# Two layers of experts behind an attention: weights of the first layer moved behind the slots' transposes, zero rows written one at a time, attention's tail a turn further ahead

## Chip, core and metric

The kernel runs on one core of a Trainium2 chip. The metric is the device time of one execution in microseconds; the kernel before takes 1737.48 us, the median of three runs (1734.93 to 1743.86). The engines are TensorE (PE; its weight loads are PEld), VectorE (DVE), ScalarE (ACT), GpSimd (POOL) and SyncE (SP). Each runs its own instructions in order; SP issues nearly all DMAs here, POOL the indirect ones.

## The reference

Three stages of 24576 tokens with 128 features each: an attention against 768 pooled keys, and two mixtures of eight experts that pick one expert per token.

```python
# attention, q (2, 12288, 128), kv (2, 384, 32, 128)
kv_pool = kv.reshape(B, H // 4, 4, W // 4, 4, C).mean(axis=(2, 4))
k = v = kv_pool.reshape(B, -1, C) @ w_sr            # 768 keys of each batch
s = (q @ k.transpose(0, 2, 1)) / sqrt(C)
a = exp(s - max(s)); a /= a.sum(-1) + 1e-9
x = (a @ v).reshape(B * S, D)
# layer 1
logits = x @ w_gate
e = argmax(logits); gate = softmax(logits)[e]
x = gate * (relu(x @ w1[e]) @ w2[e])                # F = 1024
# layer 2: the same, with logits = cosine(x, expert_emb) / tau and its own w1, w2
```

## The kernel before

**Attention** runs over 48 groups of 512 tokens. Its work is written as a list `plan` of entries `operation:lag`; in turn n an entry does its operation for group n - lag. The letters that matter here are `K` (scores, line 531), `N` (row maximum), `E` (exponential), `S` and `Z` (high and low half of the probabilities in fp16), `t` (DMA transpose on SP, line 568), `A` (product with v, lines 575 to 577), `R` (product with `iwg`: output and logits, line 603), `p` (one small step of the routing, whose last four steps are scatters of rows by POOL, line 491) and `ul`, `ua`, `ug`, `uw`, which prepare layer 1's expert weights. The largest lag is 6, so the last group is done in turn 53.

**Routing.** Each token's row (its value as two fp16 halves, its gate and its number) is scattered into an HBM table `xs` at a row that belongs to its expert. For each layer two tables of slots are made on the chip (`table`, kinds "a" and "b"); kind "b" also writes 512 zero rows behind the last row of each expert (`zrows`, line 799), eight writes of 260 KB. A table is a generator that takes one step at each `.` of the plans (eight in a slot's turn), or all at once when a slot needs it.

**Slots.** A slot is 512 (a few times 256) rows of one expert, 50 in layer 1 and 51 in layer 2, numbered from 1 in the instructions' names (x0_9 is the ninth, of layer 0 in the program's counting). A slot's work is in three lists, `both`, `plan_1` and `plan_2`, each cut into eight parts by "/"; entries are merged by their position in a turn. `X` loads a slot's rows by a DMA transpose (`x`, line 930), `W0` and `W1` load its weights (line 868; skipped at run time where the buffer holds the expert already), `H` and `h`, `g` are relu(x w1) for one of eight blocks of 128 hidden features (TensorE lines 955 to 957, ScalarE 960, VectorE 965), `Y` the second product (974 to 976), `p` the steps after it. In layer 1 these begin with the two halves of the result and two DMA transposes of them (`rowss`, line 1000); `n` are the norms: POOL adds the transposed halves (line 1012), ScalarE squares them (line 1017).

**Weights.** Expert weights are prepared in five phases: load the raw fp32 weights into `wraw` (`pw_load`, two DMAs of 512 KB, lines 340 and 341), square both halves (ScalarE, line 350), take a power of two from the sums, split each half into fp16 high and low parts in `whl` (ScalarE line 358, VectorE line 374), store them (`pw_store`, lines 383 and 385, 1 MB). `wraw` and `whl` have one buffer each. Layer 1's experts 0 to 4 are done during attention, 5 to 7 during the slots, by the entries `vl`, `va`, `vg`, `vs` of `plan_1`, and layer 2's eight after them; for layer 2 only the scales are stored, and the slots split the weights themselves.

**The seam.** Attention's last turns run among the first slots: after each entry of the slots' lists the program emits attention's entries up to position `n0 + i + m / len(plan_l) + DN` (in turns, n0 = 48, `DN` = 0). Four rules force attention further where a PSUM bank is shared: slot 0's `H0` waits for the last `E`, `Y0` and `p` of the first slots for the last `x`, `l` and `w`; `upto` then emits all entries up to that one at once. The order in which the program emits instructions is the order in which each engine runs them.

Of the kernel before, what the change touches and what calls it, by code (L numbers as in the profile page):

```python
# [66 lines left out]
def moe_kernel(tc, q, kv, w_sr, w_gate, w1a, w2a, emb, tau, w1b, w2b, out):  # L67
    with ExitStack() as ctx:
        _body(ctx, tc, q, kv, w_sr, w_gate, w1a, w2a, emb, tau, w1b, w2b, out)


def _body(ctx, tc, q, kv, w_sr, w_gate, w1a, w2a, emb, tau, w1b, w2b, out):
# [272 lines left out]
    def pw_square(i, k):  # L345
        raw = pw[i][0]
        if k == 0:
            pw[i][1] = sm.tile([P, 2], F32, tag="wss", name=f"wss{i}", bufs=2)
            pw[i][3] = p1.tile([P, WC], F16, tag="whl", name=f"whl{i}")
        A.activation(pw[i][3].bitcast(BF16)[:, 0:F], raw[:, k, :], AF.Square, accum_out=pw[i][1][:, k:k + 1])  # L350

    def pw_act(i, ph):
        raw, ss, sc, hl = pw[i]
        if ph == 1:
            pw_square(i, 1)
        elif ph in (3, 4) and i < E:
            k = ph - 3
            A.activation(hl[:, 2 * F * k:2 * F * k + F], raw[:, k, :], AF.Copy, scale=sc[:, k:k + 1])
# [18 lines left out]
    def pw_store(i, ph):  # L377
        if ph == 0:
            pw_square(i, 0)
        if ph == NPH - 1:  # L380
            l, e = divmod(i, E)
            _, _, sc, hl = pw.pop(i)
            ins = [SP.dma_start(WS[l][e * P:(e + 1) * P, :], sc).ins]
            if l == 0:
                ins.append(SP.dma_start(WT[e * P:(e + 1) * P, :], hl).ins)
                if e >= EA:
                    for w in ins:
                        for r in w_reads:
                            tc.declare_no_dep(w, r, reason="weights of other experts")
                    w_late.extend(ins)  # L390
# [248 lines left out]
    def at_u(g, fn):  # L639

        i, ph = divmod(g - U0, UP)
        if 0 <= i < EA and ph % UW == 0 and ph // UW < NPH:
            fn(i, ph // UW)


    def table(info, l, kind, ns, nh=0, prev=None, left=None):
# [24 lines left out]
        def slots_of(lim):  # L671

            cmp = tt([P, E, NG], "cmp")
            n = tt([P, E], f"n{lim}")
            V.scalar_tensor_tensor(cmp, todo.unsqueeze(2).to_broadcast([P, E, NG]), float(-lim),
                                   kidx.unsqueeze(1).to_broadcast([P, E, NG]), op0=ALU.add, op1=ALU.is_gt)
            yield
            V.tensor_reduce(n, cmp, axis=AX.X, op=ALU.add)
            yield
            return n  # L680
# [63 lines left out]
        n = yield from slots_of({"a": TG - 0.5, "b": TG // 2, "c": 0}[kind])  # L744
# [51 lines left out]
        if kind != "a":  # L796
            for e in range(E):
                r = sp_val(bi[0:1, e:e + 1], NROW - TG)
                ins = SP.dma_start(XS[l].rows[bass.ds(r, TG), :].rearrange("(p r) c -> p r c", r=4), zrows)
                XS[l].wrote(ins.ins)  # L800
                if e % 2:
                    yield
            info["upto"] = XS[l].mark()
        if kind == "b":
            lf = tt([P, E], "lf")
# [17 lines left out]
    def sp_val(ap, hi):  # L823
        return nc.values_load(ap, engines=[mybir.EngineType.SP], min_val=0, max_val=hi,
                              skip_runtime_bounds_check_because=SKIP)
# [312 lines left out]
    for n, ((i, w0, m), t) in enumerate(zip(parts, tl)):  # L1138
# [13 lines left out]
        if n == 6:  # L1152
# [7 lines left out]
    steps = {"q": at_q, "Q": at_Q, "qH": at_qH, "qL": at_qL, "K": at_K, "N": at_N, "E": at_E, "S": at_S, "D": at_D,  # L1160
             "Z": at_Z, "t": at_t, "A": at_A, "x": at_x, "r": at_r, "R": at_R, "w": at_w, "l": at_l, "o": at_o, "p": at_p,
             "ul": lambda g: at_u(g, pw_load), "ua": lambda g: at_u(g, pw_act),
             "ug": lambda g: at_u(g, pw_dve), "uw": lambda g: at_u(g, pw_store)}
    plan = """
        q:0 K3:3 ul:0 S1:3 p:6 Z3:4 E2:3 p:6 p:6 A5:5 qL:2 p:6 . ua:0 N3:3 t2:4 p:6 ug:0 w1:6 x:5 o0:6 Q:1 p:6 K0:2
        p:6 o1:6 Z1:3 R0:5 N0:2 t0:3 E3:3 R1:5 p:6 p:6 S2:3 t3:4 E0:2 S0:2 kd:1 kg:0 . l0:5 l1:5 K1:2 r0:3 Z2:3 p:5
# [15 lines left out]
    def at_turn(n):  # L1182

        for m, x in enumerate(plan):
# [24 lines left out]
            if 0 <= g < NG and not (g == 0 and o in ("Q", "qH", "qL")) and not (o == "q" and g < 3):  # L1209
                steps[o](g) if k is None else steps[o](g, k)  # L1210
                done.add((g, o, k))
                if o == "p" and g == G_A - 1 and NA1 and st[g]["post"].gi_frame is None and "l" not in taba:
                    taba["l"] = 0
                    side.append(table(taba, 0, "a", NA1))
                    tick()
                yield m

    def pw_all(steps_):
        for i in steps_:
            for fn in (pw_load, pw_act, pw_dve, pw_store):  # L1220
                fn(*divmod(i, NPH))

    def turns(slots, hooks, after, first_part=None):
# [46 lines left out]
    def run(*a):  # L1270
        for _ in turns(*a):
# [2 lines left out]

    lsteps = {"X": slot_load, "f": slot_mark, "W": slot_w, "H": slot_h, "h": slot_hH,
              "g": slot_hL, "Y": slot_y, "B": slot_raw, "C": slot_hi, "D": slot_lo}
    wsteps = {"vl": pw_load, "va": pw_act, "vg": pw_dve, "vs": pw_store}

    both = """
        Y3:3 h6:3 H7:3 g6:3 . / Y4:3 h7:3 H0:2 g7:3 . / Y5:3 h0:2 H1:2 g0:2 . / Y6:3 h1:2 H2:2 g1:2 . /  # L1280
        Y7:3 h2:2 H3:2 g2:2 f:2 . / Y0:2 h3:2 H4:2 g3:2 . / Y1:2 h4:2 H5:2 g4:2 . / Y2:2 h5:2 H6:2 g5:2 ."""
    plan_1 = """
        - - p:5 p:4 n:5 - p:4 p:4 / W0:1 n:4 p:5 p:4 n:5 - p:5 p:4 p:5 p:4 / X:1 vl:0 p:5 n:5 - p:5 n:4 vg:1 n:4 p:4 /
        - n:4 p:5 n:4 - p:4 p:4 p:4 / - n:4 p:5 - p:4 - vs:1 / p:3 W1:1 n:4 p:5 - - n:4 /
        - p:3 p:3 n:4 p:3 - n:4 va:0 n:4 / - n:4 p:3 - n:4 p:4 - n:4"""
    plan_2 = """
        - - p:4 - D3:2 / - - - - / - - p:4 - X:1 / - - - - C0:1 p:4 / - - - - D0:1 C1:1 / p:3 - - p:3 - - D1:1 /
        - - B0:0 - C2:1 - D2:1 / - - B1:0 - C3:1 -"""
# [11 lines left out]
    def first(info, l, n):  # L1300
        return lambda: side.append(table(info, l, "a", n))

    def rest(info, l, n_a, prev=None, left=None):
        side.append(table(info, l, "b", NG - n_a, NH[l], prev.get("rows") if prev else None,
                          left["left"] if left else None))
# [8 lines left out]
            before[e] = ins  # L1314

    last_a = NG + max(lags)
    DN = 0

    along = NA1 and NA2

    def late():
        if not NA1:
            pw_all(range(min(NPH * E, max(0, NG - U0)), NPH * E))
        if not along:
            pw_all(range(NPH * E, 2 * NPH * E))
# [22 lines left out]
    if NA1:  # L1348
# [8 lines left out]
        def upto(what):  # L1357
            nonlocal pos
            while what not in done:
                pos = next(rest_)  # L1360

        for i, m, j, o in turns(slots, hooks, after, NPH * E if along else None):
# [7 lines left out]
            if j == 0 and o == "p":  # L1370
                upto((NG - 1, "l", 1))
                upto((NG - 1, "w", 1))
            while pos < (n0 + i + m / len(plan_l) + DN) * len(plan):
                pos = next(rest_, 1 << 30)
# [5 lines left out]
    n = nc.values_load(tab2b["count"][0:1, 0:1], min_val=0, max_val=2 * NT, skip_runtime_bounds_check_because=SKIP)  # L1380
# [31 lines left out]
```

## Time and profile before

| what | value |
|---|---|
| median of three runs | 1737.48 us |
| profiled execution, its own time | 1748.93 us |
| its span, first to last instruction | 1747.2 us |
| busy: PE, DVE, ACT, POOL | 1594.9, 1441.0, 1328.0, 982.0 us |
| mean granted TensorE clock | 0.975 |
| DMA | 240.61 MB, mean 138 GB/s |

The profile is one execution; the span is 1.7 us shorter than the execution's time. A busy share is a mean over stages, so the rows below go by stretches of the span, in us from its start: attention until about 600, its tail among the first slots until about 690, layer 1's slots until about 1230, layer 2's slots to the end. A matmul's duration in the trace includes its pipeline, so a slot's time is better taken from the distance of slot starts than from the sum of its matmuls. A wait is put down to the last of the things waited for.

### The profile page before, as it was taken

The page shows a single profiled execution, that of the slowest core. Times are in us where ns is not written, and L with a number is a line of the kernel's source. Part 1 is how long each engine was busy: PE and PEld are TensorE (multiplying, and loading weights), DVE is VectorE, ACT ScalarE, POOL GpSimd, SP SyncE. Part 2 cuts the span into 40 slices and gives each one's busy share as a digit, 9 for nine tenths or more (in the row PEclk, how much of TensorE's full clock was granted, in tenths as well). Part 3 has the DMA queues.
Part 4 walks back from the last instruction along what each step waited for, and adds up shares of the span by engine and source line. Part 5 has one row for each costly group of instructions (what it writes and reads, how often), then busy time and mean ns, then how long its engine had stood idle before and what let it go on. Part 6 is the DMA issues. An engine that isn't in the chain of part 4 may idle for free.

```text
span 1747.2 us, 31671 instructions
## 1 busy us (share of the span) xinstructions
PE 1594.9 (91%) x8713; PEld 890.4 (51%) x8713; DVE 1441.0 (82%) x3887; ACT 1328.0 (76%) x2731; POOL 982.0 (56%) x1298
## 2 busy tenths in 40 slices
PE   6888988989888789899999999998999999999996
PEld 6666656656666534444444444444444444444443
DVE  5898989989899757787788787787998888888875
ACT  3777778878777746776777877776888888888885
POOL 1386665665565646565666666665544444444453
PEclk9899999999999999999999999999999999999998
DMA  7999998999999953444665455445337335343353
GB/s 247 218 236 201 173 225 174 207 209 179 218 181 190 189 108 78 110 109 113 145 160 123 98 112 106 74 95 128 76 77 175 78 76 127 75 83 74 77 121 63
DMA packets 631019, 240.61 MB, mean 138 GB/s; under 512 B 578464, under 2 KB 604202, under 8 KB 629168
## 3 DMA queue, kind: packets, MB, share of 16 engines
q1 hardware_dynamic: 611776, 200.31, 57.5%
q0 software_dynamic: 18752, 38.18, 8.2%
q8 instruction: 70, 1.15, 0.3%
q14 instruction: 117, 0.96, 0.2%
q10 hardware_dynamic: 304, 0.01, 0.0%
HBM read 148.53 MB, written 52.02 MB: 115 GB/s over the span
## 4 chain that ended last, share of the span: by engine, by line
PE 57%; DVE 18%; issue 8%; DMA 7%; ACT 6%; POOL 3%; SPq 0%; POOLq 0%; ACTq 0%; DVEq 0%
PE ps L957 7%; PE ps L955 7%; PE ps L974 7%; PE ps L956 7%; PE ps L976 7%; PE ps L975 7%; PE ps L531 5%; DVE hL L965 4%; DMA aT<-ab 3%; DVE ab L561 3%; DMA rowss<-yHLs 2%; DVE nm L538 2%; PE ps L575 2%; ACT ab L552 2%; PE ps L577 2%
## 5 line engine op out<-in xcount | busy, mean ns | idle before, releaser
L965 DVE SCALAR_TENSOR_TENSOR hL<-ps,hH 128x512 f16<-128x512 f32 (+1 forms) x808 | 540.0, 672 | 168.6 <-ACT hH L960 114.6
L960 ACT ACTIVATE hH<-ps 128x512 f16<-128x512 f32 (+1 forms) x808 | 466.7, 584 | 174.4 <-PE ps L957 144.2
L1075 POOL DMA_INDIRECT out_dram<-rowss,idxs x198 | 211.4, 1068 | 258.9 <-DVE idxs L1072 157.7
L974 PE MATMUL ps<-hH,wbuf 128*128 128x512 f16 (+1 forms) x808 | 304.1, 376 | 7.3 <-ACT hH L960 7.1
L491 POOL DMA_INDIRECT xs<-rowsa,idxa x192 | 202.6, 1055 | 189.5 <-DVE sca L431 143.1
L976 PE MATMUL ps<-hL,wbuf 128*128 128x512 f16 (+1 forms) x808 | 303.9, 376 | 1.3
L975 PE MATMUL ps<-hH,wbuf 128*128 128x512 f16 (+1 forms) x808 | 304.0, 376 | 0.0
L957 PE MATMUL ps<-x,wbuf 128*128 128x512 f16 (+1 forms) x808 | 304.0, 376 | 0.0
L955 PE MATMUL ps<-x,wbuf 128*128 128x512 f16 (+1 forms) x808 | 304.0, 376 | 0.0
L956 PE MATMUL ps<-x,wbuf 128*128 128x512 f16 (+1 forms) x808 | 303.8, 376 | 0.0
L491 POOL DMA_INDIRECT xs<-rowss,idxs x196 | 204.9, 1046 | 61.6 <-issue 26.8
L545 ACT ACTIVATE a<-ps,nm 128x768 f32<-128x768 f32 x192 | 171.9, 896 | 64.2 <-DVE nm L538 63.1
L561 DVE SCALAR_TENSOR_TENSOR ab<-a,ab 128x768 f16<-128x768 f32 x192 | 201.1, 1047 | 9.9 <-ACT ab L552 9.9
L538 DVE TENSOR_REDUCE nm<-ps 128x1 f32<-128x768 f32 x192 | 181.4, 945 | 32.6 <-PE ps L531 17.9
L552 ACT ACTIVATE ab<-a 128x768 f16<-128x768 f32 x192 | 161.1, 839 | 32.2 <-DMA aT<-ab 28.0
L918 DVE SCALAR_TENSOR_TENSOR wbuf<-wbuf,wsl 128x512 f16<-128x512 f32 x204 | 151.9, 745 | 0.0
L575 PE MATMUL ps<-aT,v 128*128 128x512 f16 x288 | 112.9, 392 | 42.8 <-DMA aT<-ab 33.2
L910 ACT ACTIVATE wbuf<-wbuf,wsl 128x512 f16<-128x512 f32 x204 | 146.0, 716 | 4.7 <-DMA wbuf<-in_moe_w_dram 4.6
L531 PE MATMUL ps<-kH,qH 128*128 128x384 f32 x384 | 129.4, 419 | 9.9 <-ACT a L545 8.8
L975 PEld LDWEIGHTS <-wbuf 128*128 128x128 f16 x808 | 79.4, 98 | 94.5 <-issue 11.3
L976 PEld LDWEIGHTS <-wbuf 128*128 128x128 f16 x808 | 79.4, 98 | 92.6 <-issue 2.2
L957 PEld LDWEIGHTS <-wbuf 128*128 128x128 f16 x808 | 79.4, 98 | 92.5 <-issue 2.2
(391 smaller groups left out, 2892.9 us busy)
## 6 DMA issues: line engine op xcount, KB each, us to landing
wbuf<-in_moe_w_dram SPq DMA_DIRECT2D x102, 512.0 KB
wbuf<-wt SPq DMA_DIRECT2D x98, 512.0 KB
wraw<-in_moe_w_dram SPq DMA_DIRECT2D x32, 512.0 KB
q<-in_q_dram SPq DMA_DIRECT2D x48, 256.0 KB
wt<-whl SPq DMA_DIRECT2D x8, 1024.0 KB
kv<-in_kv_dram SPq DMA_DIRECT2D x12, 512.0 KB
xs<-zrows SPq DMA_DIRECT2D x18, 260.0 KB
out_dram<-rowss,idxs POOLq DMA_INDIRECT x198
```

The costliest lines, as they stand in the source:

```text
L491: ins = G.indirect_dma_start(out=XS[l].rows, out_offset=bass.IndirectOffsetOnAxis(ap=idx[:, r:r + 1], axis=0), in_=rows[:, r, 0:RW], in_of ...
L531: PE.matmul(sv[:, h, :], lhsT=d[x][:, P * t:P * (t + 1)], rhs=k[:, 384 * h:384 * (h + 1)], start=k is kH and x == "qH", stop=x == "qL")
L538: V.tensor_reduce(d["nm"][:, t:t + 1], scores(g, t), axis=AX.XY, op=ALU.max, negate=True)
L561: V.scalar_tensor_tensor(ab[:, 1, :], st[g].pop(("a", t)), AS, ab[:, 0, :], op0=ALU.mult, op1=ALU.subtract)
L955: PE.matmul(hb, lhsT=wL, rhs=s.xH, start=True, stop=False)
L956: PE.matmul(hb, lhsT=wH, rhs=s.xH, start=False, stop=False)
L957: PE.matmul(hb, lhsT=wH, rhs=s.xL, start=False, stop=True)
L960: A.activation(hH, ps[:, f % 4, 0:s.W], AF.Relu)
L965: V.scalar_tensor_tensor(hL, ps[:, f % 4, 0:s.W], 0.0, s.h[f][0], op0=ALU.max, op1=ALU.subtract)
L974: PE.matmul(s.acc, lhsT=wL, rhs=hH, start=f == 0, stop=False)
L975: PE.matmul(s.acc, lhsT=wH, rhs=hH, start=False, stop=False)
L976: PE.matmul(s.acc, lhsT=wH, rhs=hL, start=False, stop=f == NF - 1)
```

## The change

1. `pw_store` is cut in two: the square of the first half stays at `vs`, the store is a new entry `vt` (`pw_out`). In `plan_1` the load `vl:0` and `W1:1` move from the turn's third and sixth part to its eighth, `vt:1` stands just ahead of the load, all three behind the last `p:3`, which issues the second `rowss` transpose. During attention load and store stay where they are.
2. After each zero-row write the table's generator yields twice; before, it yielded once after two writes.
3. `DN` is 1.0.

```diff
     def pw_act(i, ph):
+        if ph == 0:
+            return
         raw, ss, sc, hl = pw[i]
...
     def pw_store(i, ph):
         if ph == 0:
             pw_square(i, 0)
+
+    def pw_out(i, ph):
         if ph == NPH - 1:
...
                 ins = SP.dma_start(XS[l].rows[bass.ds(r, TG), :].rearrange("(p r) c -> p r c", r=4), zrows)
                 XS[l].wrote(ins.ins)
-                if e % 2:
-                    yield
+                yield
+                yield
...
-             "ug": lambda g: at_u(g, pw_dve), "uw": lambda g: at_u(g, pw_store)}
+             "ug": lambda g: at_u(g, pw_dve), "uw": lambda g: (at_u(g, pw_store), at_u(g, pw_out))}
...
-    wsteps = {"vl": pw_load, "va": pw_act, "vg": pw_dve, "vs": pw_store}
+    wsteps = {"vl": pw_load, "va": pw_act, "vg": pw_dve, "vs": pw_store, "vt": pw_out}
...
     plan_1 = """
-        - - p:5 p:4 n:5 - p:4 p:4 / W0:1 n:4 p:5 p:4 n:5 - p:5 p:4 p:5 p:4 / X:1 vl:0 p:5 n:5 - p:5 n:4 vg:1 n:4 p:4 /
-        - n:4 p:5 n:4 - p:4 p:4 p:4 / - n:4 p:5 - p:4 - vs:1 / p:3 W1:1 n:4 p:5 - - n:4 /
-        - p:3 p:3 n:4 p:3 - n:4 va:0 n:4 / - n:4 p:3 - n:4 p:4 - n:4"""
+        - - p:5 p:4 n:5 - p:4 p:4 / W0:1 n:4 p:5 p:4 n:5 - p:5 p:4 p:5 p:4 / X:1 p:5 n:5 - p:5 n:4 vg:1 n:4 p:4 /
+        - n:4 p:5 n:4 - p:4 p:4 p:4 / - n:4 p:5 - p:4 - vs:1 / p:3 n:4 p:5 - - n:4 /
+        - p:3 p:3 n:4 p:3 - n:4 va:0 n:4 / - n:4 p:3 vt:1 vl:0 W1:1 n:4 p:4 - n:4"""
...
-    DN = 0
+    DN = 1.0
```

The order of instructions, at the three places that matter. Line numbers of the changed kernel are four higher behind the new function. First SP's queue in a turn in which expert 5 is stored and expert 6 loaded (`wraw6`, `wt`; `wbuf01` and `wsl0` are what `W1` loads; `rowss0_7` is slot 7's transpose), before:

```order
L340 DMA wraw6_8669<-in_moe_w1_dram 128x1024
L341 DMA wraw6_8669<-in_moe_w2_dram 128x8x128
L383 DMA ws0_141<-wsc5_8286 128x4
L385 DMA wt_140<-whl5_7937 128x4096
L868 ISA
L868 DMA wbuf01_6247<-wt_140 128x2048
L868 ISA
L868 DMA wsl0_6248<-ws0_141 128x4
L1000 DMA_TRANSPOSE rowss0_7_8766<-yHLs0_7_8742 128x4x128 x2
```

and in the changed kernel:

```order
L1004 DMA_TRANSPOSE rowss0_7_8759<-yHLs0_7_8737 128x4x128 x2
L387 DMA ws0_141<-wsc5_8286 128x4
L389 DMA wt_140<-whl5_7951 128x4096
L340 DMA wraw6_8800<-in_moe_w1_dram 128x1024
L341 DMA wraw6_8800<-in_moe_w2_dram 128x8x128
L872 ISA
L872 DMA wbuf01_6247<-wt_140 128x2048
L872 ISA
L872 DMA wsl0_6248<-ws0_141 128x4
```

The two `rowss` transposes, the last of nine rows before, are now the first; the store comes ahead of the load.

Second SP's queue at attention's last transpose (`aT47`, of `ab47_3`), among the loads of the first slots (`wbuf` weights, `x0_` rows), before:

```order
L824 TENSOR_LOAD t0ai0a_6242 x2
L868 ISA
L868 DMA wbuf00_6246<-wt_140 128x2048
L824 TENSOR_LOAD t0ai0a_6242
L930 ISA
L930 DMA_TRANSPOSE x0_3_7411<-xs0_138 128x2x512
L932 ISA
L932 DMA gt0_3_7412<-xs0_138 128x4x4
L568 DMA_TRANSPOSE aT47_7235<-ab47_3_7287 128x12x128
L868 ISA
```

and in the changed kernel:

```order
L934 DMA_TRANSPOSE x0_2_7322<-xs0_138 128x2x512
L936 ISA
L936 DMA gt0_2_7323<-xs0_138 128x4x4
L572 DMA_TRANSPOSE aT47_7229<-ab47_3_7248 128x12x128
L872 ISA
L872 DMA wbuf1_7306<-wt_140 128x2048
L872 ISA
L872 DMA wsl1_7307<-ws0_141 128x4
L828 TENSOR_LOAD t0ai0a_6242 x2
L872 ISA
L872 DMA wbuf00_6246<-wt_140 128x2048
```

It stood behind `wbuf00` for the third slot and that slot's rows `x0_3`; now it stands ahead of both, behind `x0_2`.

Third POOL's queue at the four scatters of attention's last group (`rowsa47`, `idxa47`), with the scatters of the first slot (`rowss0_1`) and the additions `y32s0_` of line 1012, before:

```order
L491 DMA xs1_139<-rowss0_1_7599,idxs0_1_7739 201216x260 x2
L1019 TENSOR_TENSOR nrs0_2_7796<-n2s0_2_7795,half_122 128x4
L491 DMA xs1_139<-rowss0_1_7599,idxs0_1_7739 201216x260
L938 TENSOR_SCALAR gate0_4_7934<-gt0_4_7681,wsl1_7214 128x4
L491 DMA xs1_139<-rowss0_1_7599,idxs0_1_7739 201216x260
L491 DMA xs0_138<-rowsa47_7531,idxa47_7949 201216x260 x3
L1030 TENSOR_TENSOR gqs0_2_7799<-gate0_2_7465,qs0_2_7797 128x4
L491 DMA xs0_138<-rowsa47_7531,idxa47_7949 201216x260
L422 COPY rowss0_3_7970<-gt0_3_7412 128x4
L1012 TENSOR_TENSOR y32s0_3_8053<-rowss0_3_7970 128x512
```

and in the changed kernel (line 1012 is line 1016 there, 491 is 495):

```order
L1016 TENSOR_TENSOR y32s0_1_7665<-rowss0_1_7597 128x512
L627 TENSOR_TENSOR rowsa47_7507<-xs47_7521,rowsa47_7507 128x2x128
L466 TENSOR_SCALAR rowsa47_7507<-sa47_7576,vs1_270 128x4
L627 TENSOR_TENSOR rowsa47_7507<-xs47_7521,rowsa47_7507 128x2x128
L476 TENSOR_TENSOR ua47_7692<-ua47_7692,oha47_7567 128x32
L1023 TENSOR_TENSOR nrs0_1_7623<-n2s0_1_7622,half_122 128x4
L942 TENSOR_SCALAR gate0_3_7745<-gt0_3_7489,wsl0_6248 128x4
L495 DMA xs0_138<-rowsa47_7507,idxa47_7755 201216x260 x2
L1034 TENSOR_TENSOR gqs0_1_7626<-gate0_1_7367,qs0_1_7624 128x4
L495 DMA xs0_138<-rowsa47_7507,idxa47_7755 201216x260 x2
L426 COPY rowss0_2_7770<-gt0_2_7323 128x4
L1016 TENSOR_TENSOR y32s0_2_7860<-rowss0_2_7770 128x512
```

Eight scatters stood between the additions of slots 2 and 3; now attention's four stand between those of slots 1 and 2.

## Rows read from the trace of the kernel before

**Rows 1.** Busy time by stage (window, length, busy us and instructions of each engine).

```profile
core 0: us, PE busy (x) PEld busy (x) DVE busy (x) ACT busy (x) POOL busy (x), PEclk, DMA share, GB/s
...
596.00:690.00 94.00, 80.04 (x437) 40.10 (x436) 59.62 (x191) 52.15 (x122) 50.09 (x74) 0.95 0.56 109
690.00:865.00 175.00, 158.99 (x914) 73.35 (x912) 139.10 (x541) 123.39 (x326) 105.04 (x140) 0.97 0.49 114
...
1230.00:1690.00 460.00, 459.87 (x2134) 208.66 (x2133) 387.63 (x724) 402.73 (x626) 216.82 (x257) 1.00 0.45 93
```

**Rows 2.** Windows of line 957 alone, cut at slot starts; eight LDWEIGHTS make a slot.

```profile
core 0: us, PE busy (x) PEld busy (x), PEclk, DMA share, GB/s
610.65:650.00 39.35, 6.03 (x17) 1.56 (x16) 0.96 0.54 102
671.75:688.60 16.85, 3.56 (x9) 0.89 (x8) 0.80 0.26 60
723.05:737.80 14.75, 2.99 (x9) 0.78 (x8) 1.00 0.51 91
785.30:803.00 17.70, 3.67 (x9) 0.89 (x8) 0.81 0.47 79
825.15:837.75 12.60, 3.02 (x9) 0.78 (x8) 1.00 0.39 84
849.35:864.10 14.75, 3.47 (x9) 0.83 (x8) 0.88 0.44 98
864.10:875.05 10.95, 3.06 (x9) 0.78 (x8) 1.00 0.93 166
875.05:1154.15 279.10, 75.74 (x201) 19.51 (x200) 1.00 0.54 110
```

**Rows 3.** The first of these windows, of lines 575 and 603, in that order.

```profile
610.65:650.00 39.35, 5.12 (x12) 1.32 (x12) 0.96 0.54 102
...
610.65:650.00 39.35, 2.91 (x20) 2.68 (x20) 0.96 0.54 102
```

**Rows 4.** SP's timeline: start, time, line, operation, out<-in.

```profile
628.34 0.10 SPq L868 DMA_DIRECT2D wbuf<-wt  x1
...
651.56 0.50 SPq L340 DMA_DIRECT2D wraw<-in_moe_w_dram  x1
...
654.69 3.07 SPq L1000 DMA_TRANSPOSE rowss<-yHLs  x2
...
660.57 1.25 SPq L930 DMA_TRANSPOSE x<-xs  x1
...
714.93 0.36 SPq L340 DMA_DIRECT2D wraw<-in_moe_w_dram  x1
...
718.16 4.83 SPq L1000 DMA_TRANSPOSE rowss<-yHLs  x2
```

**Rows 5.** Chain of waits: start, time, what.

```profile
630.89 3.81 DMA aT<-ab
...
720.36 7.04 DMA rowss<-yHLs
```

**Rows 6.** Waits from 690 to 865 us: total, times, longest; then SP's.

```profile
POOL y32s L1012 <- DMA rowss<-yHLs: 39.5, 14, 7.3
...
ACT sqs L1017 <- POOL y32s L1012: 14.7, 4, 5.3
...
SPq L340 <- DVE whl L374: 6.2, 3, 2.3
```

**Rows 7.** ScalarE's timeline, the first square of new weights.

```profile
664.53 1.05 ACT L350 ACTIVATE whl<-wraw 128x1024 bf16<-128x1024 f32 x1
```

**Rows 8.** SP's timeline, the zero rows.

```profile
811.60 5.14 SPq L799 DMA_DIRECT2D xs<-zrows  x6
```

**Rows 9.** POOL's timeline at the slot of 671.75 us.

```profile
669.84 0.98 POOL L491 DMA_INDIRECT xs<-rowsa,idxa  x1 [0.30 <-DVE s2s L1034]
...
674.92 1.16 POOL L1012 TENSOR_TENSOR y32s<-rowss 128x512 f32<-128x512 f16 x1
```

More of the change, by code (lines that the diff above doesn't have):

```diff
@@ L1219, in pw_all @@
         for i in steps_:
-            for fn in (pw_load, pw_act, pw_dve, pw_store):
+            for fn in (pw_load, pw_act, pw_dve, pw_store, pw_out):
                 fn(*divmod(i, NPH))
```

## The prediction

> **What bounds the kernel now.** I read the stages first (the view by windows). From 1230 to 1690 us, layer 2's slots, TensorE is busy 459.87 of 460 us: nothing hides there and nothing is to be had. The two stretches where layer 1 begins are different: 596 to 690, where attention's tail runs among the first slots, has 80.04 of 94 us busy, and 690 to 865 has 158.99 of 175 [rows 1]. No other engine is full in either, so what the change can win lies in these 30 us of idle TensorE and in a lower clock beside them. The second view counts line 957, which runs eight times in each slot, over windows cut at slot starts: the last column of counts, LDWEIGHTS, says how many slots a window holds. From 875 to 1154 us 25 slots take 279.10 us, 11.16 each; that is my base. One slot at 671.75 takes 16.85, those at 723.05, 785.30 and 849.35 take 14.75, 17.70 and 14.75, and the one at 825.15 takes 12.60 [rows 2]. Five slots thus carry 5.7 + 3.6 + 6.5 + 3.6 + 1.4 = 20.8 us over the base, part of it as matmuls at the low clock level (granted clock 0.80, 0.81 and 0.88 in three of the windows, where 0.5 is 1.2 GHz and 1.0 is 2.4 GHz), after idle time of TensorE.
>
> Then I asked who is late. In SP's own timeline the load of an expert's raw weights (two DMAs of 512 KB) stands at 714.93, with the previous expert's store (1 MB) behind it and the post step's two transposes, `rowss`, only behind that, at 718.16 [rows 4]. The chain of waits has that transpose under way from 720.36 for 7.04 us [rows 5]. The waits of 690 to 865 us say who pays: POOL's addition L1012 waits 39.5 us for it in 14 slots, 2.8 on average and 7.3 at the longest; ScalarE's squares behind it wait 14.7 us, in only 4 cases, up to 5.3 each; and ScalarE runs in order, so the slot's `hH` and with them TensorE stand still. SP itself waits 6.2 us in 3 cases at the load, line 340, for VectorE's last use of the raw tile [rows 6].
>
> **The change part by part.**
>
> *Load and store behind the transposes.* Nothing is removed: per expert two loads, a small store and for layer 1 the 1 MB store are issued as before, on the same queue, about five eighths (load) and two eighths (store) of a turn later. `vg:1` now precedes the load in the turn, so the three waits of 6.2 us in all have no cause left, and the transposes stand ahead of 2 MB instead of behind. The three slots at 723, 785 and 849 us can lose their 3.6 + 6.5 + 3.6 = 13.7 us. What is late next? First, ScalarE's square of the new weights. In the turn of 650 us the transposes are issued at 654.69 and take SP until 657.76; with the two small issues of the store behind them the load would start at some 659, and the first square stands at 664.53, 5.5 us later; today that load is issued at 651.56, 13 us ahead of it [rows 4, 7]. How long do 2 MB take? From 714.93 to the transposes' landing at 727.40 are 12.5 us [rows 4, 5], with two transposes of about 3 us in it, so 9.4 us for 2 MB and 7 for the 1.5 MB that end with the first half of the load: the square is 1.5 us late, at worst (all 2 MB) 3.9, at best (store and load beside each other) not at all. Second, the next slot's transpose `x`, issued at 660.57 for a slot that starts at 671.75 [rows 2, 4]: behind 2 MB it lands at 659 + 9.4 + 3 = 671.4, just in time. I take 1.5 us for each of the three events, since the first square is the nearer of the two: 13.7 - 4.5 = 9.2 us gained. The ends are 13.7 and 13.7 - 3 x 3.9 = 2.0.
>
> The queue's behaviour has a page: by the Trainium skill (DMA: Bandwidth & Descriptors, "Queues, rings and completion order") each DMA engine takes the descriptors of one ring in order. That agrees with the 7.04 us of a transpose behind 2 MB, and by it alone the whole 13.7 us would go.
>
> For layer 2's eight experts there is a load of 1 MB and no large store. The base of 11.16 holds seven of them; the slot at 864.10, between two loads, took 10.95 [rows 2], so 25 x 0.21 = 5 us is the most that they cost now. A load half as large had five eighths of a turn to drain ahead of the transposes, so I take 1 us, with -1 (a square late) to 5 as ends. `W1` moves behind the transposes in all layer-1 slots; most are skipped (same expert as two slots before), a real one still has six eighths of a turn before `Y0`: nothing, within the same ends.
>
> *Zero rows singly.* Eight writes of 260 KB; six of them stand in one run from 811.60 for 5.14 us of SP time [rows 8], ahead of the next `x` and `rowss`, and the slot at 825.15 takes 1.4 us more than the base [rows 2]. Spread over two turns they leave at most two together: 1.2 us gained, ends 0 and 1.4. In layer 2 the last writes now come just ahead of the first slot that reads behind them; that slot starts a turn of 10 us later, which hides a landing: nothing.
>
> *Attention's tail a turn ahead.* No instruction is added. Two places count. (a) POOL. At 669.84 four scatters of attention's last group follow four of a slot, and the addition L1012 starts at 674.92 [rows 9], where the slot's squares, and TensorE, wait: the slot at 671.75 loses 5.7 us [rows 2]. In the new order these four stand a slot earlier, between two additions that have no slot scatters between them, so POOL has four scatters of about 1.0 us in each turn and not eight. I take 4.5 of the 5.7 (ends 0 and 5.7). (b) The two slots from 610.65 to 650 take 39.35 us [rows 2], 17.0 over the base. Of this the 12 x 3 attention matmuls of 512 columns, at the slots' pace of 11.16 / 48 = 0.23 each, are 8.3 and the products with `iwg` 2.9 [rows 3]: 5.8 us are idle or at the low clock. One piece: attention's last transpose is issued at 630.89 and lands 3.8 us later, and TensorE's next product waits for it [rows 5]; it stands behind a slot's weight load that went out at 628.34 only [rows 4], since its buffer was in use by TensorE. Now it stands ahead of that load. The other piece is the burst that the rules at `Y0` and `p` force out; it is now emitted in its place. Against this, the turn with attention's 46th group has no slot matmuls in it any more: the four first products of slot 0, 12 x 0.23 = 2.8 us, stand behind, and while TensorE waits for the transposes its clock may drop, which doubles the time of the 18 matmuls behind (4.1 us more at the most). I take 4 us gained, nearer to the upper end because the one row at hand, the transpose behind the load, is a wait that the order removes; ends 5.8 and -5 (the 2.8 lost and half of the clock's 4.1, with none of the 5.8 back).
>
> **Sum.** 9.2 + 1.0 + 1.2 + 4.5 + 4.0 = 19.9 us. The profiled execution took 1748.93 us for a span of 1747.2 and is 11.5 us above the median of the three runs, 1737.48; from it 1729.0 would be left. The stalls are waits of fixed length and not shares, so I take the same 19.9 off the median: 1717.6, forecast 1717.5. The good ends sum to 13.7 + 5 + 1.4 + 5.7 + 5.8 = 31.6 (1705.9), the bad ones to 2.0 - 1 + 0 + 0 - 5 = -4.0 (1741.5). All bad ends together are unlikely, so the range is 1703 to 1738, its lower end left a little beyond the sum for a clock that no longer drops.
>
> **Rivals.**
> 1. *The square waits in the transposes' place.* For it: the load has 5.5 us where it had 13. Against it: only half of it must be there, and ScalarE in 690 to 865 us is not full. The events give 2.0, the rest its 10.7: 12.7 gained, 1724.8. The Trainium skill (same page, "Rules for kernel authors") says to issue a DMA early and wait late, which speaks for this rival; no run here shows it yet.
> 2. *The tail wins nothing.* The gap at the transposes of group 46, now without slot products to fill it, eats what the POOL order gives: -5 + 4.5 = -0.5, with the rest 11.4 - 0.5 = 10.9, and if the POOL scatters only collide a slot earlier, 6.4: 1726.6 to 1731.
> 3. *Slower: the `x` transposes become the late transfer.* Place: the turn behind each event, where `x` queues behind store and load. If 2 MB take the full 12.5 us from 714.93 to 727.40, `x` lands at 659 + 12.5 + 3 = 674.5 against a need at 671.75, and the square is 7 us late: each event then costs 7 us where it costs 4.6 now, so 3 x 2.4 = 7 us are lost, with the tail's -5 12 us: 1749. It decides once store, load and one transpose together need more than 12 us. Against it: in those 12.5 us the transposes are contained.
> 4. *The change does nothing on the clock*: the bubbles go, but ScalarE and VectorE, at 123 and 139 of 175 us [rows 1], set the same slot time: 1735. Against it: undisturbed slots take 10.95 with the same engines.
>
> **How the numbers follow.** Forecast as summed 0.58; rival 1 0.18; rival 2 0.13; rival 3 0.06; rival 4 0.05. About 0.5% of 1737.5, 8.7 us, is what a measurement can tell from no change, so the line is 1728.8. The forecast and rival 1 lie below it but for their edges (0.70 of 0.76), rival 2 half (0.07): faster 0.77. Same: the edges, half of rival 2, rival 4: 0.16. Slower: rival 3 with a little of the rest: 0.07.
>
> **What would show it.** Right: line 340 gone from SP's waits; no ScalarE wait for L1012 over 3 us between 690 and 865; the slots that hold an event at 11 to 13 us; POOL's four attention scatters ahead of slot 1's addition; no run of six zero writes. Wrong: a wait of ScalarE's line 350 for the load, an `x` that TensorE waits for in the turn after an event, or more idle TensorE between 600 and 620 us than before.

## The result, and the profile after

The changed kernel takes 1722.71 us (median of seven runs, 1719.45 to 1729.26); the kernel before, run beside it, 1742.53 us (seven runs, 1734.93 to 1748.26). The ratio is 0.9892, 95% interval 0.9868 to 0.9916: 19.8 us or 1.1% faster. Five more runs of the changed kernel on the chip of the last experiments gave 0.9885 (0.9870 to 0.9900). Forecast were 19.9 us and 1717.5 us. The profiled execution took 1720.96 us for a span of 1719.2.

By stage, as in [rows 1] (the same columns; the slots now start earlier in the span, so each stretch begins later in the work):

```profile
core 0: us, PE busy (x) PEld busy (x) DVE busy (x) ACT busy (x) POOL busy (x), PEclk, DMA share, GB/s
596.00:690.00 94.00, 85.85 (x494) 42.16 (x494) 69.53 (x224) 59.80 (x148) 57.76 (x81) 0.98 0.56 108
690.00:865.00 175.00, 164.92 (x980) 77.84 (x978) 146.85 (x571) 130.25 (x347) 113.27 (x152) 1.00 0.60 135
```

TensorE is idle for 18 us of these 269 where it was for 30, and the granted clock in the second stretch is 1.00 (2.4 GHz) where it was 0.97. The slots that answer to [rows 2], again by the third matmul of the first product (line 961 now): the first two slots, the one that held attention's last scatters before, the one with the zero rows; then the three with an event (an expert's store and load), and the 25 behind them.

```profile
core 0: us, PE busy (x) PEld busy (x), PEclk, DMA share, GB/s
612.45:640.30 27.85, 6.07 (x16) 1.56 (x16) 1.00 0.46 91
662.95:673.90 10.95, 3.03 (x8) 0.78 (x8) 1.00 0.35 73
803.30:814.40 11.10, 3.03 (x8) 0.78 (x8) 1.00 0.61 168
...
708.90:720.90 12.00, 3.03 (x8) 0.78 (x8) 1.00 0.83 219
768.00:780.20 12.20, 3.00 (x8) 0.78 (x8) 1.00 0.97 220
826.00:838.50 12.50, 3.03 (x8) 0.78 (x8) 1.00 0.83 211
849.50:1129.90 280.40, 76.20 (x201) 19.50 (x200) 1.00 0.53 111
```

The scatters' slot went from 16.85 to 10.95, the events' slots from 14.75, 17.70 and 14.75 to 12.00, 12.20 and 12.50, the zero rows' from 12.60 to 11.10. The 25 slots behind, which hold seven of layer 2's loads, did not get faster (279.10 before). The granted clock is 1.00 in all of these windows, where it was 0.80 to 0.96 in four of them before.

Who waits from 690 to 865 us (total, times, longest), to be set beside [rows 6]:

```profile
POOL y32s L1016 <- DMA rowss<-yHLs: 24.7, 15, 2.5
...
ACT whl L350 <- DMA wraw<-in_moe_w_dram: 4.4, 4, 1.6
```

POOL's longest wait for a transpose fell from 7.3 to 2.5 us, ScalarE's wait for POOL's addition from 14.7 us in all to 0.7, and SP's at line 340 is gone. One wait is new, ScalarE's for the raw weights. SP's timeline and then ScalarE's show how it comes, beside [rows 4, 7]:

```profile
701.50 5.32 SPq L1004 DMA_TRANSPOSE rowss<-yHLs  x2
706.87 0.57 SPq L387 DMA_DIRECT2D ws<-wsc  x1
707.49 0.44 SPq L389 DMA_DIRECT2D wt<-whl  x1
707.97 0.56 SPq L340 DMA_DIRECT2D wraw<-in_moe_w_dram  x1
708.58 1.21 SPq L341 DMA_DIRECT2D wraw<-in_moe_w_dram  x1
...
714.02 1.06 ACT L350 ACTIVATE whl<-wraw 128x1024 bf16<-128x1024 f32 x1 [0.92 <-DMA wraw<-in_moe_w_dram]
```

The load goes out at 707.97, behind the transposes and the store, and the square starts 6.05 us later, having waited 0.92 us. On POOL attention's last scatters (`rowsa`) now stand in a gap of their own, unlike [rows 9]:

```profile
640.46 1.15 POOL L1016 TENSOR_TENSOR y32s<-rowss 128x512 f32<-128x512 f16 x1 [2.32 <-DMA rowss<-yHLs]
...
646.03 1.09 POOL L495 DMA_INDIRECT xs<-rowsa,idxa  x1 [1.20 <-issue]
...
650.09 0.97 POOL L495 DMA_INDIRECT xs<-rowsa,idxa  x1 [0.30 <-issue]
651.21 1.16 POOL L1016 TENSOR_TENSOR y32s<-rowss 128x512 f32<-128x512 f16 x1
...
654.47 1.00 POOL L495 DMA_INDIRECT xs<-rowss,idxs  x1 [0.62 <-ACT sqs L1021]
```

And the run of six zero writes [rows 8] is gone: at most two stand together.

```profile
797.13 1.89 SPq L803 DMA_DIRECT2D xs<-zrows  x2
...
802.52 0.34 SPq L803 DMA_DIRECT2D xs<-zrows  x1
...
809.02 1.20 SPq L803 DMA_DIRECT2D xs<-zrows  x2
```

The two spans differ by 28.0 us, more than the medians. I cut both, and every profile below, at four marks: the end of attention's last score product (line 531 before), and the first matmuls of the sixth slot, of layer 1's last slot (the 50th) and of layer 2's third.

| stretch, us | before | changed | changed, second profile |
|---|---|---|---|
| start to last score product | 607.4 | 600.3 | 607.0 |
| to the sixth slot | 81.1 | 73.7 | 75.0 |
| to layer 1's last slot | 506.6 | 495.5 | 496.6 |
| to layer 2's third slot | 37.1 | 35.9 | 36.0 |
| to the end | 514.9 | 514.0 | 514.5 |

Up to the first mark the program of the engines is nearly the same, and its length varies from profile to profile, 600.3 and 607.0 us in two of one kernel. So the 7 of the 28 us that lie there can't be put down to the change. Whether none of them belongs to it is open: over all profiles the mark lies at 597.9 to 607.0 us in the changed kernel and its four variants, and at 605.5 to 611.3 in the eight without the whole change. Behind the mark the change gave 20.6 us in the first profile and 17.6 in the second, where the medians say 19.8 and 20.3.

### The profile page after: what moved, and what is told of

Read it like the earlier page. It is cut to its first block, busy times and chain, and to the rows that moved or that the text cites. A ratio compares the mean times of both kernels' runs of the same rounds, so it can differ in the third digit from the quotient of the medians.

```text
span 1719.2 us, 31621 instructions
## 1 busy us (share of the span) xinstructions
PE 1580.1 (92%) x8713; PEld 886.9 (52%) x8713; DVE 1440.2 (84%) x3887; ACT 1325.7 (77%) x2731; POOL 989.6 (58%) x1298
## 4 chain that ended last, share of the span: by engine, by line
PE 54%; DVE 19%; issue 9%; DMA 8%; ACT 6%; POOL 3%; SPq 0%; POOLq 0%; DVEq 0%; ACTq 0%
PE ps L959 7%; PE ps L978 7%; PE ps L961 7%; PE ps L960 7%; PE ps L979 7%; PE ps L980 7%; DMA aT<-ab 5%; DVE ab L565 4%; PE ps L535 4%; DVE hL L969 3%; DVE nm L542 3%; ACT ab L556 2%; PE ps L579 1%; PE ps L581 1%; PE ps L580 1%
## 5 line engine op out<-in xcount | busy, mean ns | idle before, releaser
L565 DVE SCALAR_TENSOR_TENSOR ab<-a,ab 128x768 f16<-128x768 f32 x192 | 201.0, 1047 | 10.4 <-ACT ab L556 10.3
```

The costliest lines, as they stand in the source:

```text
L565: V.scalar_tensor_tensor(ab[:, 1, :], st[g].pop(("a", t)), AS, ab[:, 0, :], op0=ALU.mult, op1=ALU.subtract)
```

## The experiments

Each ratio is against the kernel before, run on the same chip in the same series: medians 1746.25 us for the three parts alone, 1746.82 for the runs with one transfer moved, the late square and two turns, 1746.48 for the split store and the combinations.

**The three parts alone.** The kernel before with one part each, and the kernel before again:

```diff
-    DN = 0
+    DN = 1.0
```

> The kernel before with attention's tail one turn ahead and nothing else. Theory (the parts add up, each at its own place): the two first slots and the slot of POOL's eight scatters lose their stalls, some 14 us by slot starts, ratio to before 0.992; the three slots with an expert's store and load keep 14.5 to 17.7 us each. Rival (the tail wins nothing by itself, the gap without slot products eats it): 0.999 to 1.003, with slot 2 starting no earlier than before.

The second has the cut `pw_store`, `vt` and the new `plan_1` of the diff, without the rest:

> The kernel before with load, store and W1 behind the transposes and nothing else. Theory: the three event slots fall from 14.5 to 17.7 us to about 12.3 each, 10 us in all, ratio 0.994; ScalarE's square waits some 1.5 us for the load. Rival (the stall only changes its place, to the square or to the next slot's x): the three slots and those behind them keep their sum, ratio 0.998 to 1.002.

```diff
-                if e % 2:
-                    yield
+                yield
+                yield
```

> The kernel before with the zero rows written singly and nothing else. Theory: one slot near 825 us falls from 12.6 to about 11.2 us, the slot before it gains half a us, about 1 us in all, ratio 0.999 to 1.000. Rival (zero rows cost as much as a weight event, about 4 us): 0.9975.

> The kernel before, unchanged, for a second profile. Theory (the profiled execution of before was a long one, 1748.9 against a median of 1742.5, by stalls that vary): slot starts differ from the first profile by some 6 us, and the difference lies in a few slots with waits. Rival (executions differ by the clock over the whole span): the difference grows evenly over the slots.

| kernel | median us | ratio (95%) | to the sixth slot | three event slots | to layer 1's last slot |
|---|---|---|---|---|---|
| before (beside the changed kernel) | 1742.53 | – | 81.1 | 47.2 | 506.6 |
| before again (one run) | 1747.58 | – | 83.0 | 46.8 | 506.2 |
| tail alone | 1737.12 | 0.9948 (0.9926 to 0.9970) | 75.6 | 44.4 | 504.1 |
| weights alone | 1736.76 | 0.9949 (0.9932 to 0.9965) | 77.1 | 37.9 | 498.3 |
| zero rows alone | 1744.25 | 0.9989 (0.9973 to 1.0004) | 79.2 | 45.5 | 505.3 |
| changed (against 1742.53) | 1722.71 | 0.9892 (0.9868 to 0.9916) | 73.7 | 36.8 | 495.5 |

The losses of ratio, 0.52, 0.51 and 0.11%, add up to 1.14%, the whole shows 1.08; each is known to some 0.2% only, so the times can't tell parts that add up from parts that overlap by a few us. The tail alone gave less than the 0.992 expected of it: the first two slots start 14.2 us behind the last score product where it was 3.2, and the stretch to the sixth slot is 5.5 us shorter, where some 14 us were expected by slot starts. The zero rows alone can't be told from nothing by time, but their slot went from 12.6 to 11.5 us. The events' slots answer to the weights. The two profiles of the kernel before differ as was expected, by up to 3 us in single slots with waits (the first two events' slots are 14.8 and 17.7 us in one, 16.9 and 15.6 in the other), while the three together differ by 0.4. One row was not foreseen: the slot that before takes 16.85 us, put down to POOL's scatters, takes 10.95 with the tail alone, but also only 12.95 with the weights alone, where the scatters are where they were. In that turn the load of expert 5, at 651.56, stood ahead of the slot's transposes [rows 4]. The window of the slot, first with the tail alone, then with the weights alone:

```profile
672.95:683.90 10.95, 3.03 (x8) 0.78 (x8) 1.00 0.35 73
```

```profile
670.15:683.10 12.95, 3.03 (x9) 0.78 (x8) 1.00 0.34 77
```

**Which transfer ahead of the transposes costs.** The kernel before with `pw_store` cut and only one of the two moved, `W1` in its old place in both: the load behind the transposes and the store in its old place (`vs:1 vt:1`), or the store behind and the load in its old place (`vt:1` where the changed kernel has it, `vl:0` behind `X:1`).

> The kernel before with the load alone moved behind the transposes; the store keeps its place ahead of them, tail and zero rows as before. Measure: the sum of the three event slots, 46 to 47 us before and 37.9 with load, store and W1 moved. Theory (the transposes wait for the bytes that stand ahead of them): half the bytes, about half the gain, 41 to 43 us, ratio to before 0.997. Rival (SP's wait of 2.1 us at the load for VectorE is the cause, which is gone here): all the gain, about 38 us, ratio 0.9945.

> The kernel before with the store alone moved behind the transposes; the load keeps its place in the turn's third part, with its wait for VectorE. Theory (bytes ahead): 41 to 43 us in the three event slots, ratio 0.997, as for the load alone. Rival (SP's wait at the load): no gain, 46 us, ratio 1.000.

Load moved alone: 1734.37 us, 0.9927 (0.9898 to 0.9956), event slots 33.9 us. Store moved alone: 1737.84 us, 0.9947 (0.9928 to 0.9966), event slots 33.5. The theory of both missed. Either edit takes away the whole stall of the events, and more of it than both together (37.9). The store-only kernel's event slots, and its waits from 690 to 865 us:

```profile
721.45:733.00 11.55, 3.03 (x8) 0.78 (x8) 1.00 0.62 160
780.65:791.75 11.10, 3.03 (x8) 0.78 (x8) 1.00 0.73 145
839.40:850.30 10.90, 3.06 (x9) 0.78 (x8) 1.00 0.61 147
```

```profile
POOL y32s L1016 <- DMA rowss<-yHLs: 26.2, 14, 5.4
...
ACT sqs L1021 <- POOL y32s L1016: 3.5, 2, 2.6
...
SPq L340 <- DVE whl L376: 6.5, 3, 2.3
```

SP still waits 6.5 us at line 340, at no cost to the slots, so SP's wait, which by the load-only run alone could have been the cause, was not. Nor is the cost in proportion to the bytes ahead. POOL's longest wait in this list, 5.4 us, is not behind the load: it stands at 817.87, behind six zero writes in a row, which this kernel still has. In the event slots, with 1 MB ahead, POOL waits 2.92, 2.06 and 1.70 us, where it waited 6.26, 7.33 and 4.46 behind 2 MB and 1.3 to 2.0 in undisturbed slots: behind 1 MB the transposes are hardly late. With both moved the last transfer issued, the load, is late for ScalarE's square instead. What the load ahead does cost is the scatters' slot: 16.40 us in the store-only kernel, 12.9 in the load-only one. No run put the transposes on another queue, so whether their place in this queue made them late, or the transfers still under way on the same DMA engines, stays open.

**Between 1 and 2 MB.** The store-only kernel with the store split, its first half ahead of the transposes (a new entry `vh:1` behind `vs:1`), the second behind:

```diff
+            ins = SP.dma_start(WT[i * P:(i + 1) * P, 0:2 * F], pw[i][3][:, 0:2 * F]).ins
...
-        - n:4 p:5 n:4 - p:4 p:4 p:4 / - n:4 p:5 - p:4 - vs:1 / p:3 W1:1 n:4 p:5 - - n:4 /
+        - n:4 p:5 n:4 - p:4 p:4 p:4 / - n:4 p:5 - p:4 - vs:1 vh:1 / p:3 W1:1 n:4 p:5 - - n:4 /
```

> The kernel before with its store split in two: the first half (0.5 MB) goes out ahead of the slot's transposes, beside the load's 1 MB, and the second half behind them, so 1.5 MB stand ahead of the transposes where the kernel before has 2 MB and the variants with one edit have 1 MB. Theory (a slack: POOL's addition may come up to some 5 us late before ScalarE and TensorE stand still, which 1 MB just fits and 2 MB does not): the three slots with an event take together between the variants' 33.7 and the kernel before's 47.2 us, 38 to 41, ScalarE waits in 1 to 3 cases of 1 to 3 us for POOL's addition, and the ratio to the kernel before is 0.995 to 0.998. Rival 1 (bytes ahead decide in proportion): 40.5 as well, but then 1 MB should not have been free. Rival 2 (any half of the traffic behind the transposes is enough): below 35, ratio 0.9945.

```profile
724.55:737.70 13.15, 3.04 (x9) 0.78 (x8) 1.00 0.66 117
785.15:799.15 14.00, 3.03 (x8) 0.78 (x8) 1.00 0.68 104
846.60:858.40 11.80, 3.03 (x9) 0.78 (x8) 1.00 0.59 119
```

```profile
ACT sqs L1032 <- POOL y32s L1027: 8.9, 4, 3.3
```

Event slots of 38.95 us, between 33.5 at 1 MB and 47.2 at 2 MB, two fifths of the way. Of ScalarE's 4 waits three are in the event slots (up to 3.3 us) and one at the zero rows. So there is a slack, but of another size than the expectation's 5 us, as POOL's and then ScalarE's timelines show, for 2 MB (before), 1.5 (this kernel) and 1 (store-only, two additions in event slots and the one behind the zero writes):

```profile
790.92 1.15 POOL L1012 TENSOR_TENSOR y32s<-rowss 128x512 f32<-128x512 f16 x1 [7.33 <-DMA rowss<-yHLs]
...
792.10 0.31 ACT L1017 ACTIVATE sqs<-y32s 128x128 f32<-128x128 f32 x1 [5.33 <-POOL y32s L1012]
...
788.92 1.16 POOL L1027 TENSOR_TENSOR y32s<-rowss 128x512 f32<-128x512 f16 x1 [5.49 <-DMA rowss<-yHLs]
...
790.11 0.31 ACT L1032 ACTIVATE sqs<-y32s 128x128 f32<-128x128 f32 x1 [3.34 <-POOL y32s L1027]
...
722.66 1.15 POOL L1016 TENSOR_TENSOR y32s<-rowss 128x512 f32<-128x512 f16 x1 [2.92 <-DVE cnts L445]
...
723.85 0.31 ACT L1021 ACTIVATE sqs<-y32s 128x128 f32<-128x128 f32 x1 [0.92 <-POOL y32s L1016]
...
780.97 1.16 POOL L1016 TENSOR_TENSOR y32s<-rowss 128x512 f32<-128x512 f16 x1 [2.06 <-DMA rowss<-yHLs]
...
817.87 1.25 POOL L1016 TENSOR_TENSOR y32s<-rowss 128x512 f32<-128x512 f16 x1 [5.37 <-DMA rowss<-yHLs]
```

In the event slots ScalarE's square waits 2.0 to 2.2 us less than POOL did: 5.33 for 7.33, 3.34 for 5.49, 0.92 for 2.92, nothing for 2.06; behind the zero writes, where POOL waited 5.37, it waits 2.56. The readers thus bear a POOL wait of about 2 us, and only what exceeds it reaches ScalarE and TensorE. The time does not follow: 1745.95 us, 1.0003 (0.9988 to 1.0018), no gain where 0.2 to 0.5% was expected. Behind the first mark this profile is 11 us shorter than before's, but the mark itself lies at 611.3 us, the latest of all. The split also halves the stores of experts 0 to 4 during attention; that this costs there is likely, but no run separates it.

**The new wait.** The changed kernel with the square of the first half, `vs:1`, two eighths of a turn later, next to `va:0`:

```diff
-        - n:4 p:5 n:4 - p:4 p:4 p:4 / - n:4 p:5 - p:4 - vs:1 / p:3 n:4 p:5 - - n:4 /
-        - p:3 p:3 n:4 p:3 - n:4 va:0 n:4 / - n:4 p:3 vt:1 vl:0 W1:1 n:4 p:4 - n:4"""
+        - n:4 p:5 n:4 - p:4 p:4 p:4 / - n:4 p:5 - p:4 - - / p:3 n:4 p:5 - - n:4 /
+        - p:3 p:3 n:4 p:3 - n:4 vs:1 va:0 n:4 / - n:4 p:3 vt:1 vl:0 W1:1 n:4 p:4 - n:4"""
```

> The changed kernel with the first square moved from the turn's fifth part to its seventh, just ahead of the second. Theory (what is left of the event slots, 36.8 us against three times 11.2, is ScalarE's wait of up to 1.6 us for the load, 4.4 us in 4 cases): the waits fall below 1 us in all, the three slots to 34 to 35.5 us, ratio to before 0.988. Rival (the rest has other causes): 36 to 37 us, ratio unchanged at 0.989.

The wait at line 350 fell from 4.4 us to 0.9 and the event slots from 36.8 to 32.9, so the new wait costs some 4 us there. The time was 1727.81 us, 0.9898 (0.9868 to 0.9927), no different from the changed kernel's. From the sixth slot to layer 1's last it takes 495.2 us where the changed kernel takes 495.5 and 496.6, so nearly all of the 4 us come back in other slots, some 2 of them among those between the events; why is not shown.

**The tail a second turn ahead**, `DN = 2.0` in the changed kernel:

> The changed kernel with attention's tail two turns ahead instead of one. Measure: time from attention's last score product to the start of slot 5, 79 to 83 us before, 73.7 in the changed kernel. Theory (a slot's products are needed to fill attention's last turns; one turn less of them is enough to take the collisions away): 75 to 79 us, ratio to before 0.991 to 0.993. Rival (each turn ahead takes more stalls away): 70 us or less, ratio 0.987.

1721.78 us, 0.9865 (0.9838 to 0.9893). From the last score product to the sixth slot 73.6 us, as with one turn (73.7), outside what either theory gave (75 to 79, or 70 and less); the ratio can't be told from the changed kernel's.

**Combinations.** The load back in its early place while the store stays behind; the same with two turns; and the changed kernel as it is:

```diff
-... X:1 p:5 n:5 ...   vt:1 vl:0 W1:1
+... X:1 vl:0 p:5 n:5 ...   vt:1 W1:1
```

> The changed kernel with one thing put back: an expert's load of raw weights goes out in the slot's third part, ahead of the transposes, as in the kernel before, while the store stays behind them. Theory: 1 MB ahead of the transposes is free and the load has its 13 us again, so ScalarE's wait for the raw weights (line 350, 4.4 us in the changed kernel) goes; the three slots with an event take 33 to 34 us instead of 36.8, and the ratio to the kernel before is 0.987 to 0.988, 2 to 4 us below the changed kernel's. Rival: with the load ahead, the slot where attention's last scatters lie (12.9 us and 10.9 with the load behind, 16.4 with it ahead and the old tail) pays 2 to 5 us again, and the ratio is 0.989 or above.

> The same as the kernel with the early load, with attention's tail one more turn ahead (a lead of 2 instead of 1). Theory: as without, within 0.2%, since the second turn of lead moved nothing from the stretch between attention's last score product and slot 5 (73.6 against 73.7 us). Rival: a load ahead of the transposes makes the scatters' turn the late one again, and a second turn of lead takes it away: 3 us faster than with a lead of 1, ratio 0.985 to 0.986.

> The changed kernel, unaltered, on the same chip as the three others, to compare them with it. Both theories: ratio 0.987 to 0.9915, a span within 4 us of 1719; the attention stage ends between 600 and 608 us, since its end differed by that much between profiles of kernels that are alike up to there.

| kernel | median us | lowest, highest | ratio (95%) | to the sixth slot | event slots |
|---|---|---|---|---|---|
| changed, again | 1726.20 | 1723.67, 1730.80 | 0.9885 (0.9870 to 0.9900) | 75.0 | 37.0 |
| early load | 1726.46 | 1725.62, 1727.45 | 0.9888 (0.9872 to 0.9904) | 74.0 | 33.6 |
| early load, two turns | 1720.50 | 1716.47, 1723.62 | 0.9856 (0.9838 to 0.9874) | 72.1 | 34.5 |

With the early load the wait at line 350 is gone from the list (two waits at line 1042, 2.7 us, are put down to the load instead) and SP's at line 340 is back with 4.3 us, the event slots (first fence below) are as short as expected, and the scatters' slot stays at 10.9 us: both causes were needed for the whole of that slot's stall. The time is that of the changed kernel all the same; 3.4 us were to be had and the two intervals are each over 5 us wide. The second turn makes the first two slots 20.20 us instead of 27.15 (second fence), but they start 5.9 us later behind the last score product.

```profile
715.05:726.70 11.65, 3.03 (x8) 0.78 (x8) 1.00 0.60 158
773.65:784.90 11.25, 3.03 (x8) 0.78 (x8) 1.00 0.65 146
831.45:842.20 10.75, 3.03 (x8) 0.78 (x8) 1.00 0.56 148
```

```profile
621.70:641.90 20.20, 6.09 (x17) 1.56 (x16) 1.00 0.34 75
```

The last kernel beat both: every one of its five runs lies below every run of its two neighbours, if by no more than 0.05 us at the nearest. Its ratio lies where its rival put it, but the gain over the early load with one turn, 6.0 us, is twice the rival's 3, and not for the rival's reason, since the slot that the rival names is undisturbed without it. Against the kernel with the early load and one turn its profile is 6.0 us shorter, as its median is: 3.0 us ahead of the first mark and 3.1 behind. Whether the first half is an effect of the second turn on attention's last turns is open; single profiles, with a spread of 7 us there, can't show it.

## Why the prediction was right

The forecast's sum stood, and with it most of the mechanism: the stalls in the five slots and at the seam shrank where it said they would. Of two stalls, the events' and the scatters', it told the cause too simply. That the total fits to 0.1 us is luck: the terms were off by up to 1.5 us in opposite directions, the second profile gives 17.6 us behind the mark, and the ratio's interval leaves 15 to 23 us.

- **Events: 9.2 forecast, 10.4 measured** (47.2 to 36.8 us). The square's wait came as forecast, 4.4 us in 4 cases for the 4.5 taken, the square starting 6.5 us behind the store's issue at 707.49 where 7 were estimated. Rival 1, a square so late that it eats the gain, and rival 3, late `x` transposes, did not come. A wait at line 350 stood among the prediction's signs of being wrong, but its own sum had paid for it. The reason behind the stall was told too simply. The prediction took the transposes' place behind 2 MB as what costs; the runs show that 1 MB there is free at the events, and that moving either transfer would have done. By the Trainium skill (DMA: Bandwidth & Descriptors, "Queues, rings and completion order") one ring's descriptors are taken in order. The trace agrees in that the transposes come later with more ahead of them: POOL's longest wait at an event is 7.3 us behind 2 MB, 5.5 behind 1.5, 2.6 to 3.3 in the four kernels with 1, and 2.1 behind none.
- **SP's wait at line 340: gone, but never a cost.** It cost nothing in the store-only kernel, where it stays.
- **Layer-2 loads: 1 forecast, none measured.** 25 slots with these loads take 280.40 us where they took 279.10; from the 21st to the 50th slot both kernels take 320 us.
- **Zero rows: 1.2 forecast, 1.5 in the slot**, 1.1 in the kernel with that part alone.
- **The scatters' slot: 4.5 forecast, 5.9 measured**, less 0.9 in the two slots ahead of it. The four scatters stand ahead of slot 2's addition; the sign in the prediction said slot 1's. The stall had two causes, the eight scatters on POOL and the load ahead of the transposes; taking either away removes most, which is why the tail and the weights each show it alone. The prediction named only POOL.
- **The seam: 4.0 forecast, 2.5 measured**, 2.2 in the second profile. This term was mis-sized. The first two slots fell from 39.35 to 27.85 us, but start 12.2 us behind the last score product where it was 3.2. The prediction's counter-term came: TensorE waits 3.61 us for the transposes of the last group but one, with no slot products to fill the time, and seven matmuls behind that stand about 0.43 us apart, the lower clock level, where the others stand 0.22 apart. TensorE's timeline of the changed kernel:

```profile
606.64 0.59 PE L579 MATMUL ps<-aT,v 128*128 128x512 f16 x1 [3.61 <-DMA aT<-ab]
607.01 0.63 PE L580 MATMUL ps<-aT,v 128*128 128x512 f16 x1
607.44 0.64 PE L581 MATMUL ps<-aT,v 128*128 128x512 f16 x1
...
610.21 0.38 PE L580 MATMUL ps<-aT,v 128*128 128x512 f16 x1
610.42 0.38 PE L581 MATMUL ps<-aT,v 128*128 128x512 f16 x1
```

- **From span to median.** The 19.9 us were taken off the median of three runs, 1737.48; with seven runs and then more, the kernel before's medians were 1742.5 to 1746.8. That, and not the terms, is why the changed kernel's 1722.7 lies 5 us above the forecast.

The Trainium skill (DMA: Bandwidth & Descriptors, "Rules for kernel authors") says to issue a DMA early and wait for it late; of this the prediction said that no run showed it. The early load does: ScalarE's wait at line 350 is gone and the three slots take 33.6 instead of 36.8 us; in the kernel's time it doesn't show.

## What to carry to other kernels

A transfer that is late costs only what exceeds the slack of its readers, here about 2 us: before ordering a queue anew, halve what stands ahead of the late transfer and see whether the stall halves or vanishes. Look up when the longest wait of a list happened before tying it to a cause. When two causes meet in one stall, each part of a change seems to own it when tried alone, so give one stall to one part of a sum only after both have been tried. Cut profiles at marks in the program and compare the stretches; whole spans of two profiles of one kernel differed here by 10 us, half of what was to be measured.

## Not expected

Two profiles of the same program differed by 6.7 us at the end of attention, a stage with a DMA share near 1 (1.09 from 559 to 607 us in the kernel before), and by 3.0 us behind it. The 29 slots from layer 1's 21st to its 50th take 319.5 to 322.1 us in all profiles, wherever layer 2's loads stand in them.
